# Zero rows of a cache gradient in four unequal transfers, and gradient rows fetched back one by one

## The chip, the cores and the metric

The kernel runs on one core of a Trainium2 chip. The metric is the device time of one execution in microseconds, as the median of several runs. One execution is also recorded by the hardware profiler; its times are counted from the start of the profile's span.

## What is computed

The reference runs a small decode step for one token (a row `x` of 1024 values) through two rounds of two layers, and returns the output and its gradients by all inputs but one bias:

```
x = x + A(layernorm(x));  x = x + B(layernorm(x));  x = x + A(layernorm(x));  x = x + B(layernorm(x))

A: q = x @ wq                          # wq 1024 x 4096, 32 heads of 128
   k, v = the last 4096 of 32768 rows of k_cache, v_cache   # 4 heads, each for 8 query heads
   o = softmax(q k^T / sqrt(128)) v;  return o @ wo         # wo 4096 x 1024
B: h = x @ w1 + b1;  return (h * tanh(softplus(h))) @ w2    # w1 1024 x 3584, w2 3584 x 1024
```

All of it is bfloat16. The returned gradients of `k_cache` and `v_cache` (`out_2`, `out_3`) have the full shape, 4 heads x 32768 rows x 128. Only the last 4096 rows of a head can differ from zero; the 28,672 rows before them (7.3 MB for each head, 58.7 MB in all) are zeros that the kernel has to write. The gradients of the four weight matrices (`out_4` to `out_6`, `out_8`) are outer products of two pairs of rows each.

## The kernel before

The weights come in through a ring of eight SBUF slots of 1 MB (`Ring`), filled by transfers on SyncE's queue (SP) in an order that is written down ahead; a slot is filled again when its user has released it (L71). The forward pass of both rounds comes first, then the backward pass from the last layer to the first. Each weight is read by TensorE, partly after turning 128x128 blocks on TensorE (L489) and copying them back with VectorE and ScalarE. The last pass of the backward chain is `attn_bwd(0, ...)`, which goes through `wo` and then through `wq` (hooks `do1`, `dp1`, `dq1`, `dn1` are called within it). Behind it the outer products are made: `work` takes units of the queues in `todo`, each unit a matmul of two rows by two rows into PSUM (L1078, and L1129 for the caches), an evacuation to SBUF, and `store` sends the piece to HBM on SP's queue (L1050, L1055).

**The zeros.** `zt` is an SBUF tile of 128 partitions x 4096 values (8 KB per partition) that is set to zero at 110 us. The list `zjobs` cuts the zero rows of each head into seven pieces of 1 MB, in which each of the 128 partitions writes one run of 8 KB. The first piece is written half by SP earlier on, and its other half is put at the end of the list. `zeros(n, after)` takes the next `n` pieces and issues one transfer for each on GpSimd's queue (POOL, L265), behind a one-value copy (L260) that waits for `after`. The calls are spread over the kernel by hand: 56 pieces in all, 55 whole ones and the half one. The last calls are `zeros(2, ...)` in `dn1` at t = 3 and `zeros(4)` behind `attn_bwd(0, ...)`, which issues three whole pieces and the half one.

**The gradient rows.** The outer products want rows, while the backward pass holds columns. `put_by` turns the columns of OC, NA, NB and AC (both rounds, "l" = 0 and 1, beside each other) and stores them in small HBM tensors `dr_OC`, `dr_NA`, `dr_NB`, `dr_AC`. `take_back(name, base, off, step)` in `do1` at c = 1 fetches them into `ROWS` (a part of the tile W1): row l to partition base + l, as n runs of 256 bytes, with n = 32 for OC, 8 for NA and NB, 28 for AC. With `step=2`, the default, one transfer brings both rows; AC uses `step=1`, one transfer for each row. All five are issued on POOL's queue (L836). The rows that are made later (`rowize`, `rowize_f`) go by the same queue (L1041), 8 runs or 7 runs to a transfer. `twins` then copies pairs of rows to other partitions on SP's queue (L1070).

Of the kernel before, what the change touches and what calls it, by code (L numbers as in the profile page):

```python
# [15 lines left out]
P = 128  # L16
HQ = 32
DH = 128
# [3 lines left out]
G = 4  # L22
W = 4096
TD = D // P
TF = F // P
# [68 lines left out]
def kernel(  # L94
# [22 lines left out]
    nc = tc.nc  # L117
# [3 lines left out]
    ZR = Sk - W  # L121
# [9 lines left out]
    def sb(shape, dtype, name):  # L131
        return keep.tile(shape, dtype, name=name)
# [24 lines left out]
    ZC = 4096  # L157
    zt = sb([P, ZC], BF16, "zt")
# [36 lines left out]
    for hi in range(4):  # L195
        r = slice(32 * hi, 32 * hi + 32)
# [10 lines left out]
    AC = sb([P, TF, 2], BF16, "AC")  # L207
# [38 lines left out]
    zjobs = []  # L246
    for out_t in (out_2, out_3):
        for g in range(G):
            dst = out_t[0, g, 0:ZR, :].rearrange("(p r) d -> p (r d)", p=P).rearrange("p (r c) -> p r c", c=ZC)
            for k in range(dst.shape[1]):  # L250
                zjobs.append(dst[:, k, :])
    zjobs.reverse()

    pz = sb([1, 16], FP32, "pz")
# [2 lines left out]
    def zeros(n, after=None):  # L257

        if after is not None and zjobs:
            nc.gpsimd.tensor_copy(pz[0:1, pz_n[0] % 16:pz_n[0] % 16 + 1], after[0:1, 0:1])  # L260
            pz_n[0] += 1
        for _ in range(n):
            if zjobs:
                dst = zjobs.pop()
                nc.gpsimd.dma_start(dst, zt[:, 0:dst.shape[1]])  # L265


    KEEP_Q = (5, 6, 7)
# [96 lines left out]
    def to_eight(bank, buf):  # L365

        nc.vector.transpose(buf[:, 0:256], bank[:, 0:256])
        return buf[:, 0:256].rearrange("p (g m) -> p g m", m=32)[:, :, 0]
# [434 lines left out]
    def last_da(k):  # L803

        for c in (5, 6):
            if k == 0:
                da_dots(c)
            else:
                ring.release(("2", 0, c))
        if k:  # L810
            nc.gpsimd.memset(zt[:], 0.0)
            zeros(1)

    def wo_hook1(c):
        if c == 0:
            zeros(7, OC[:, 0, 1:2])
        if c:
            conv(1)
# [10 lines left out]
        DR[name] = dram.tile([2 * n, P], BF16, name=f"dr_{name}")  # L829
        nc.sync.dma_start(DR[name][:], r)  # L830

    def take_back(name, base, off, step=2):
        r = DR[name][:].rearrange("(n l) p -> l n p", l=2)
        to = ROWS[base:base + 2, off:off + r.shape[1] * P].rearrange("l (n p) -> l n p", p=P)
        for l in range(0, 2, step):
            nc.gpsimd.dma_start(to[l:l + step], r[l:l + step])  # L836

    x3, st3, sA1 = attn_fwd(1, x2, st2, False, wo_hook1, last_da)
    put_by("OC", OC, HQ)
    put_by("NA", NA, TD)  # L840
    zeros(8, x3)
    sB1 = mlp_fwd(1, x3, st3, lambda: conv(1, "A"))
    put_by("NB", NB, TD)
# [26 lines left out]
    def rowize_f():  # L870

        b = big().bitcast(BF16)
        for l in range(2):
            for k in range(4):
                nc.tensor.transpose(b[0:7, (4 * l + k) * P:(4 * l + k + 1) * P],
                                    DHC[:, :, l].rearrange("p (c k) -> p k c", k=4)[:, k], ident_bf[:])
        nc.scalar.copy(rf.rearrange("c (l p k) -> c l p k", l=2, k=4), b[0:7].rearrange("c (l k p) -> c l p k", l=2, k=4))
        for l in range(2):
            rows_out.append((ROWS[64 + l:65 + l, NOFF:NOFF + F].rearrange("o (c j) -> o c j", j=512),
                             rf[:, 512 * l:512 * l + 512]))  # L880
# [133 lines left out]
    ROWS = W1S[:, 0:5120]  # L1014
    NOFF = 1024
# [11 lines left out]
    def rowize(cols, n, base, off):  # L1027

        b = big().bitcast(BF16)
        nc.tensor.transpose(b[0:2 * n, 0:P], cols[:].rearrange("p n l -> p (n l)"), ident_bf[:])  # L1030
        k = rt_n[0]
        rt_n[0] += 1
        nc.scalar.copy(rt[0:2 * n, k, :], b[0:2 * n, 0:P])
        for l in range(2):
            rows_out.append((ROWS[base + l:base + l + 1, off:off + n * P].rearrange("o (t p) -> o t p", p=P),
                             rt[l:2 * n:2, k, :]))

    def rows_go(queue):

        while rows_out:  # L1040
            queue.dma_start(*rows_out.pop(0))  # L1041
# [144 lines left out]

    def do1(c):
        if c == 1:
            take_back("AC", 96, NOFF, 1)
            take_back("OC", 32, NOFF)  # L1190
            take_back("NB", 64, 0)
            take_back("NA", 0, 0)
        if c == 4:
            y = to_eight(YR, RT.rearrange("p a t s -> p (a t s)")[:, 0:512].bitcast(FP32))
            nc.vector.tensor_tensor(out=x4[:], in0=y, in1=x3[:], op=ALU.add)
        if c == 5:
            rowize(GA, TD, 32, 0)
            rowize(GB, TD, 96, 0)
            rows_go(nc.gpsimd)
            zeros(2)  # L1200
        if c == 6:
            rowize_f()
            rows_go(nc.gpsimd)
# [13 lines left out]
    def dn1(t):  # L1217
# [6 lines left out]
        if t == 5:  # L1224
            todo[0].append(units_cols(0, 8, out_4))

    g0_rest = attn_bwd(0, sA0, g1, ("o", 3), ("q", 3), (), dict(do=do1, dp=dp1, dq=dq1, dn=dn1))
    zeros(4)
    stage_free.extendleft(ring_t[:, i, :] for i in range(8))
    stage_free.extendleft(lent)  # L1230

# [50 lines left out]
```

## Time and profile before

| What | Value |
|---|---|
| median of 3 runs | 450.72 us (450.44 to 450.92) |
| the profiled execution | 450.31 us |
| its span | 448.5 us |
| granted TensorE clock, mean | 0.668 |
| DMA traffic in the span | 181.40 MB, mean 404 GB/s |
| busy: PE, DVE, ACT, POOL | 70%, 58%, 47%, 10% |
| the 55 whole zero pieces | 1024 KB each, 20.7 us from issue to landing (median) |

The page of the profile gives busy time by engine, the span in 40 slices of 11.2 us, the DMA queues, and the costliest groups of instructions. q1 is the queue of SP, q0 that of POOL, q10 that of ACT. "DMA" is the mean busy share of the 16 DMA engines of the core. A transfer is cut into packets (8 KB or less here), dealt out over the DMA engines, and each engine ends its part with a 4-byte packet that counts up the transfer's semaphore. A line number such as L265 is a line of the kernel as printed above.

### The profile page before, as it was taken

The numbers are of one execution on the slowest core, as the hardware profiler recorded it, in microseconds if no ns is written. First come the engines' busy times: TensorE is split into PE (matmuls) and PEld (weight loads), VectorE is DVE, ScalarE is ACT, GpSimd is POOL, SyncE is SP. The second block draws the span as 40 slices with busy tenths as digits, with TensorE's granted clock in tenths as the row PEclk, the third lists the DMA queues.
The fourth block names the chain that finished last, engine by engine and source line by source line (L and its number), as shares of the span: only waits on it lengthen the run. The fifth ranks groups of instructions, "written<-read, shape, count | busy, mean of one in ns | idle before, by whom it ended". The sixth has DMA issues, their size and how long they took to land.

```text
span 448.5 us, 12849 instructions
## 1 busy us (share of the span) xinstructions
PE 314.8 (70%) x5681; PEld 243.3 (54%) x5681; DVE 262.2 (58%) x516; ACT 209.4 (47%) x238; POOL 44.5 (10%) x94
## 2 busy tenths in 40 slices
PE   3835542565698797987987666798877888899600
PEld 3735532445685696986986545798862222234300
DVE  4504746368551664864477447654478998998600
ACT  2501101011058576861474341561348999999700
POOL 1000000001232212102101003023220000000000
PEclk9955555556559799986799657957685555555555
DMA  8999999999999999999999999999999899999994
GB/s 336 422 420 420 419 419 418 418 355 425 400 422 421 422 422 416 397 422 422 424 422 422 427 423 419 405 410 388 405 397 412 347 411 416 416 420 411 409 406 192
DMA packets 30057, 181.40 MB, mean 404 GB/s; under 512 B 3954, under 2 KB 5162, under 8 KB 12082
## 3 DMA queue, kind: packets, MB, share of 16 engines
q1 hardware_dynamic: 21478, 122.30, 66.6%
q0 software_dynamic: 8432, 58.26, 31.5%
q8 instruction: 44, 0.72, 0.6%
q14 instruction: 11, 0.09, 0.0%
q10 hardware_dynamic: 92, 0.02, 0.0%
HBM read 81.84 MB, written 98.62 MB: 402 GB/s over the span
## 4 chain that ended last, share of the span: by engine, by line
DMA 40%; PE 31%; DVE 13%; ACT 5%; issue 4%; SPq 0%; ACTq 0%; DVEq 0%
DMA ring<-in_B_w_dram 13%; PE BIG L489 10%; DMA W<-in_A_wo_dram 9%; DMA ring<-in_A_wq_dram 7%; DMA ring<-in_A_wo_dram 5%; DMA W<-in_B_w_dram 4%; PE TP L508 4%; PE wide L1129 4%; ACT ring L316 3%; PE wide L1078 3%; DVE ring L313 3%; DMA W<-in_A_k_cache_dram 2%; DVE W L313 2%; PE BIG L667 2%; PE MV L956 2%
## 5 line engine op out<-in xcount | busy, mean ns | idle before, releaser
L316 ACT COPY ring<-BIG 128x1024 bf16<-128x1024 bf16 x52 | 51.4, 1014 | 50.0 <-PE BIG L489 30.2
L1078 PE MATMUL wide<-W 2*128 2x512 bf16 x240 | 53.1, 597 | 9.7 <-ACT ring L316 2.4
L489 PE MATMUL BIG<-ident_bf,ring 128*128 128x128 bf16 x672 | 54.5, 234 | 2.0 <-issue 1.2
L489 PEld LDWEIGHTS <-ring 128*128 128x128 bf16 x768 | 51.6, 107 | 3.4 <-issue 2.7
L466 DVE CUSTOM_DVE_ANT_0 junk<-ring,SC 128x1024 bf16<-128x1024 bf16 x32 | 38.9, 1215 | 11.0 <-DMA ring<-in_B_w_dram 10.6
L1078 PEld LDWEIGHTS <-W 2*128 2x128 bf16 x240 | 12.8, 102 | 46.3 <-issue 45.4
L508 PEld LDWEIGHTS <-ring 128*128 128x128 bf16 x864 | 29.9, 98 | 11.7 <-issue 6.3
L316 ACT CAST ring<-wide 128x1024 bf16<-128x1024 f32 (+1 forms) x37 | 34.5, 1015 | 1.1 <-PE wide L1078 1.1
L265 POOL DMA_DIRECT2D out_dram<-zt x56 | 29.9, 538 | 48.8 <-DMA out_dram<-zt 47.9
L313 DVE CAST ring<-wide 128x1024 bf16<-128x1024 f32 (+1 forms) x27 | 31.3, 1198 | 2.8 <-PE wide L1078 2.7
L316 ACT COPY KT<-BIG 128x1024 bf16<-128x1024 bf16 x22 | 21.6, 1007 | 21.8 <-PE BIG L667 19.9
L313 DVE COPY ring<-BIG 128x1024 bf16<-128x1024 bf16 x32 | 21.8, 689 | 15.1 <-PE BIG L489 12.5
L466 DVE CUSTOM_DVE_ANT_0 junk<-ring,DSX 128x1024 bf16<-128x1024 bf16 x24 | 29.4, 1224 | 0.8
L489 PE MATMUL BIG<-ident_bf,W 128*128 128x128 bf16 x280 | 26.9, 255 | 3.1 <-DMA W<-in_A_wo_dram 2.7
L316 ACT COPY W<-BIG 128x1024 bf16<-128x1024 bf16 x20 | 20.1, 1014 | 11.8 <-PE BIG L489 11.6
L551 PE MATMUL MV<-NA,ring 128*128 128x1 bf16 x512 | 15.3, 165 | 13.4 <-DMA ring<-in_A_wq_dram 12.1
L489 PEld LDWEIGHTS <-W 128*128 128x128 bf16 x288 | 21.6, 123 | 3.5 <-DMA W<-in_A_wo_dram 2.9
L551 PEld LDWEIGHTS <-ring 128*128 128x128 bf16 x512 | 14.7, 104 | 14.2 <-DMA ring<-in_A_wq_dram 12.8
L1129 PE MATMUL wide<-W 32*128 32x256 bf16 x128 | 19.7, 403 | 1.5 <-DVE KT L313 0.9
L316 ACT CAST KT<-wide 128x1024 bf16<-128x1024 f32 x19 | 19.1, 1030 | 1.6 <-PE wide L1129 1.1
L316 ACT CAST W<-wide 128x1024 bf16<-128x1024 f32 x16 | 16.0, 1024 | 6.6 <-PE wide L1078 6.2
L354 PE MATMUL YR<-ring,AC 128*32 128x256 bf16 x208 | 10.9, 367 | 11.1 <-DMA ring<-in_B_w_dram 8.7
(279 smaller groups left out, 524.5 us busy)
## 6 DMA issues: line engine op xcount, KB each, us to landing
out_dram<-zt POOLq DMA_DIRECT2D x55, 1024.0 KB, 20.7
ring<-in_A_wq_dram SPq DMA_DIRECT2D x24, 1024.0 KB, 12.8
ring<-in_A_wo_dram SPq DMA_DIRECT2D x14, 1024.0 KB, 19.0
ring<-in_B_w_dram SPq DMA_DIRECT2D x13, 1024.0 KB, 18.9
W<-in_A_wo_dram SPq DMA_DIRECT2D x10, 1024.0 KB, 19.9
out_dram<-ring SPq DMA_DIRECT2D x15, 512.0 KB, 11.1
W<-in_B_w_dram SPq DMA_DIRECT2D x8, 896.0 KB, 18.4
out_dram<-ring SPq DMA_DIRECT2D x5, 1024.0 KB, 12.3
```

Source lines behind the costliest of these rows:

```text
L265: nc.gpsimd.dma_start(dst, zt[:, 0:dst.shape[1]])
L313: nc.vector.tensor_copy(dst, src)
L316: nc.scalar.copy(dst, src)
L354: nc.tensor.matmul(bank[32 * j:32 * j + 32, 0:n].rearrange("p (g a) -> p g a", a=m.shape[-1]), lhsT=vec.to_broadcast([P, 32]), rhs=m, star ...
L466: nc.vector.tensor_tensor_reduce(out=out, in0=a, in1=vec, scale=1.0, scalar=acc if i else 0.0, op0=ALU.mult, op1=ALU.add, accum_out=acc)
L489: nc.tensor.transpose(b[:, i * P:(i + 1) * P], block(w, i) if block else w[:, i * P:(i + 1) * P], ident_bf[:])
L508: nc.tensor.matmul(out, lhsT=w[:, i * P:(i + 1) * P], rhs=rhs_of(i), start=fresh[0], stop=last and i == n - 1, skip_group_check=True)
L551: nc.tensor.matmul(q_ps[:, h:h + 1], lhsT=ch[:, h * P:(h + 1) * P], rhs=NA[:, t, l:l + 1], start=(k == 0 and h == 0), stop=(k == TD - 1), ...
L667: nc.tensor.transpose(b[:, i * P:(i + 1) * P], T[:, g, 8 * b8 + i, :], ident_bf[:])
L956: nc.tensor.matmul(dq_ps[:, g_ * 8:g_ * 8 + 8], lhsT=KT[:, g_, t, :], rhs=DSX[:, c:c + 8], start=(g_ == 0 and t == 0), stop=(t == TS - 1), ...
L1078: nc.tensor.matmul(b[:, 512 * i:512 * i + 512], lhsT=R[at:at + 2, lo:lo + P], rhs=R[at:at + 2, ro + 512 * i:ro + 512 * i + 512], start=Tru ...
L1129: nc.tensor.matmul(b[:, k * 256:(k + 1) * 256], lhsT=RT[32 * g:32 * g + 32, a, tp, :], rhs=YS[32 * g:32 * g + 32, :], start=True, stop=Tru ...
```

## The change

For the last of the eight heads (`out_3`, g = 3) the zero rows are cut differently: 896 units of 32 rows (8 KB each). The first 512 units (4 MB) are set aside as `zless`; the other 384 make three ordinary pieces of 1 MB. So `zjobs` is four pieces shorter, and the call `zeros(4)` at the end becomes `zeros_less()`, which writes the 512 units with four transfers: from 4 partitions (0, 4, 8, 12) 33 units each, from partition 16 17 units, from 3 partitions (20, 24, 28) 33 each, and from 8 partitions (64, 68, ... 92) 33 each. Each partition of the tile of zeros is read again and again for its units. The half piece, last in the list, is now issued by the call in `dn1`.

`take_back` issues one transfer for each row; AC's row of 28 runs is fetched in two, of 24 and of 4 runs. That makes ten transfers in place of five, and the parameter `step` goes.

```diff
     for out_t in (out_2, out_3):
         for g in range(G):
-            dst = out_t[0, g, 0:ZR, :].rearrange("(p r) d -> p (r d)", p=P).rearrange("p (r c) -> p r c", c=ZC)
-            for k in range(dst.shape[1]):
-                zjobs.append(dst[:, k, :])
+            rest = out_t[0, g, 0:ZR, :]
+            if (out_t, g) != (out_3, G - 1):
+                dst = rest.rearrange("(p r) d -> p (r d)", p=P).rearrange("p (r c) -> p r c", c=ZC)
+            else:
+                units = rest.rearrange("(u r) d -> u (r d)", r=ZC // DH)
+                zless, dst = units[0:4 * P], units[4 * P:].rearrange("(r p) c -> p r c", p=P)
+            zjobs += [dst[:, k, :] for k in range(dst.shape[1])]
...
+    def zeros_less():
+
+        at = 0
+        for k, p, n in ((4, 0, 33), (1, 16, 17), (3, 20, 33), (8, 64, 33)):
+            nc.gpsimd.dma_start(zless[at:at + k * n].rearrange("(k n) c -> k n c", k=k),
+                                zt[p:p + 4 * k:4, None, :].to_broadcast([k, n, ZC]))
+            at += k * n
...
-    def take_back(name, base, off, step=2):
+    def take_back(name, base, off):
+
         r = DR[name][:].rearrange("(n l) p -> l n p", l=2)
-        to = ROWS[base:base + 2, off:off + r.shape[1] * P].rearrange("l (n p) -> l n p", p=P)
-        for l in range(0, 2, step):
-            nc.gpsimd.dma_start(to[l:l + step], r[l:l + step])
+        n = r.shape[1]
+        for l in range(2):
+            to = ROWS[base + l:base + l + 1, off:off + n * P].rearrange("o (n p) -> o n p", p=P)
+            for a, b in ((0, 24), (24, n)) if n == TF else ((0, n),):
+                nc.gpsimd.dma_start(to[:, a:b], r[l:l + 1, a:b])
...
-            take_back("AC", 96, NOFF, 1)
+            take_back("AC", 96, NOFF)
...
-    zeros(4)
+    zeros_less()
```

## The prediction

> **What bounds the kernel now.** I read the page first: the row of the 16 DMA engines, the queues, the byte count.
>
> ```profile
> span 448.5 us, 12849 instructions
> ...
> DMA  8999999999999999999999999999999899999994
> ...
> DMA packets 30057, 181.40 MB, mean 404 GB/s; under 512 B 3954, under 2 KB 5162, under 8 KB 12082
> ...
> q1 hardware_dynamic: 21478, 122.30, 66.6%
> q0 software_dynamic: 8432, 58.26, 31.5%
> ```
>
> The DMA engines are full in 38 of 40 slices, and thin out only in the last. The kernel is bound by 181.4 MB of traffic, of which POOL's zeros (q0) are 58 MB. The change moves the same bytes, so it can win only where engines stand idle: at the end. The table by stage, cut fine there (columns: stretch, its length, busy time of PE, weight load, DVE, ACT and POOL, clock, share of the 16 DMA engines, GB/s), shows it:
>
> ```profile
> 440.00:442.00 2.00, 0.00 (x0) 0.00 (x0) 0.00 (x0) 0.00 (x0) 0.00 (x0) 0.50 1.03 410
> 442.00:442.50 0.50, 0.00 (x0) 0.00 (x0) 0.00 (x0) 0.00 (x0) 0.00 (x0) 0.50 0.52 205
> 442.50:443.00 0.50, 0.00 (x0) 0.00 (x0) 0.00 (x0) 0.00 (x0) 0.00 (x0) 0.50 0.14 57
> 443.00:443.50 0.50, 0.00 (x0) 0.00 (x0) 0.00 (x0) 0.00 (x0) 0.00 (x0) 0.50 0.06 25
> 443.50:444.00 0.50, 0.00 (x0) 0.00 (x0) 0.00 (x0) 0.00 (x0) 0.00 (x0) 0.50 0.06 25
> 444.00:445.00 1.00, 0.00 (x0) 0.00 (x0) 0.00 (x0) 0.00 (x0) 0.00 (x0) 0.50 0.07 29
> 445.00:446.00 1.00, 0.00 (x0) 0.00 (x0) 0.00 (x0) 0.00 (x0) 0.00 (x0) 0.50 0.06 25
> 446.00:447.00 1.00, 0.00 (x0) 0.00 (x0) 0.00 (x0) 0.00 (x0) 0.00 (x0) 0.50 0.07 29
> ```
>
> No engine computes. Up to 442 all 16 DMA engines move 410 GB/s, 25.6 each; from 443 to 447 the rate is 25 to 29 GB/s, a share of 0.06: **one DMA engine works alone** for 4 us, the other 15 are done.
>
> The trace also keeps every DMA packet with start, duration, size and queue, but without its engine. The last ones give the exact end: 4096-byte packets of 159 ns, starting 155 ns apart (a packet starts 3 to 4 ns before the one ahead of it ends), the last ending at 447.16. Eleven engines end between 442.15 and 442.35, the next to last at 443.07. From the last packet to the span's end (448.54) are 1.38 us, and from the span to the execution's time (450.31) 1.77.
>
> **Which engine it is.** By that 3 to 4 ns rule packets can be chained, each 16th of a transfer in its order. From 200 to 281 us the chains are unbroken: in one, an 8192-byte packet takes 323.3 ns in the mean and 69 take over 330; in the other 15 the mean is 309.0 to 315.4, with at most 2 over 330. So one engine is slow, and it drags its zeros behind it: of POOL's last old transfer, 15 sixteenths are through at 347 and eight packets run alone from 352.5 to 354.7.
>
> The same chains show how POOL's transfers are dealt out. Transfers with one outer dimension always go to the same engines: the two 28-row fetches of AC to the same 14, two rows each, the four 8-row moves of GA and GB at 301 us to the same eight. Transfers with two outer rows (OC, NB, NA) take two engines each, and each the next two: six different ones, all among those eight. The slow engine has one of NA's two shares: the fifth or sixth in turn.
>
> **The change, part by part.**
>
> *Unequal shares.* Behind the last pass of wq, before: four transfers, 3.5 MB; after: 512 units of 8 KB in groups of 4, 1, 3 and 8 partitions, 33 units each, but 17 for the lone one. One more half-size job falls to the call ahead, so the two calls move 5.5 MB together as before. Even dealing of 512 units is 32 per engine. A unit took 309 ns and starts 305 to 306 after the one ahead. If each partition is one engine in turn from the first, the fifth has 15 units less: 15 x 0.306 = 4.59 us; the rest one more, 0.31. The slow engine then ends at 447.16 - 4.59 = 442.57, and late next is the engine of 443.07, at 443.07 + 0.31 = 443.38. The end moves by 447.16 - 443.38 = 3.78 us. Nothing is won earlier: the DMA share is 1.01 to 1.03 in all stages from 360 on.
>
> *Issues.* Four for four; one took 0.53 to 0.69 us on POOL, in the view of tile zt. They have 17 to 264 units, not 128; by count that is 0.1 to 1.4 us each. POOL has no work behind them, and at 331.6 its queue still holds transfers that land up to 355.5. I take 0; up to 2 us late costs nothing while that backlog lasts.
>
> *One partition read 33 times.* No row shows it. Below, 0: a packet read one partition before, too. Above, the slow engine's 323 instead of 309 ns: 33 x 14 = 0.46 us. I take 0, which is nearest: same packet size and direction.
>
> *Row fetches.* Five issues become ten. POOL's timeline (start, length, what, idle before it and its releaser):
>
> ```profile
> 276.92 1.04 POOL L836 DMA_DIRECT2D W<-dr_AC  x2 [5.29 <-DMA ring<-in_A_wo_dram]
> 278.00 0.70 POOL L836 DMA_DIRECT2D W<-dr_OC  x1
> 278.69 0.60 POOL L836 DMA_DIRECT2D W<-dr_NB  x1
> 279.28 0.56 POOL L836 DMA_DIRECT2D W<-dr_NA  x1
> 298.22 2.06 POOL L1041 DMA_DIRECT2D W<-W  x4 [18.38 <-ACT W L1033]
> ```
>
> Five more at 0.52 to 0.70 us are 3 us, into 18.38 us of idle. POOL has eight completion semaphores in turn, so the ninth fetch waits for the first to land (14.8 us after its issue, 291.7), the tenth likewise: POOL is free near 293. Behind it wait L1041's moves, which wait for ACT until 298.22, and SP's copies (L1070), first at 305.23. On the slow engine a data packet and its semaphore alternate with q1's 8 KB packets, 0.65 us per fetch; ten end near 297.5. Cost 0; without the cover each us behind 298.22 would delay the twins and the first stores.
>
> What the fetches do is to leave the turn alone: no transfer with two rows is left. If the turn starts each execution where it started here, the shares begin at the first engine.
>
> **Sum.** 450.31 - 3.78 = 446.53 against the profiled execution. That one lies 0.41 under the median (450.72), so I predict 446.9.
>
> **The rivals.**
>
> *A. The short share is the slow engine's*: 446.9; with the costs above up to 447.6, down to 446.3 if the spread among the others closes too. For it: the lag (447.16 - 442.3 = 4.9 us) is 16 units of 0.306, what the lone share lacks; the pair of NA. Against: fifth or sixth is open, and so is how 17 rows of one partition are dealt. 0.50.
>
> *B. The 17 units are dealt like the 28 rows of AC*, two each over nine engines from the first; then 4, 3 and 8 engines follow in turn, and the sixteenth has none. The slow engine has 35 units in place of 32: 3 x 0.306 = 0.92 us later, 451.6. It decides as soon as one outer row of 17 is treated as the AC fetches were, and they show just that. This is the rival on the other side. 0.25 with kindred ones (17 units beside 33 on one engine: 442.3 + 18 x 0.306 = 447.8, 0.65 later, 451.4).
>
> *C. The short share falls on another engine*: the sixth was the slow one, or the turn stands elsewhere (before moves it by six engines per execution; if that outlives an execution, the starting point is any). The slow engine has 33: 0.31 later, 451.0, no change. 0.20.
>
> *D. A cost I take as 0 appears*, the fetches above all: 451.5 and more, 0.05.
>
> Two rules of the Trainium skill, page "DMA: Bandwidth & Descriptors", bear on this. Its section "Why a DMA increments its semaphore by 16 and not by 1" says a transfer uses the largest k up to 16 that divides its slowest dimension, on k consecutive engines from a round-robin cursor, but that some POOL copies deal ⌈partitions/16⌉ to each. By the first, 17 rows sit on one engine (case A); by the second the sum is B's. The trace disagrees with the first for AC: 14 engines, the cursor not moved. The section "Latency and other measured facts" says engines 7 and 15 are usually the slow ones; by that the fifth share would miss, as in C. The trace has one slow engine only, in NA's pair, which contradicts it if the turn starts at the first engine.
>
> **How the numbers follow.** A is likeliest: 446.9, its own range 446.3 to 447.6. Half of the rest is on the other side, so the range goes over B: 446.3 to 451.7. Within 0.2% (0.9 us, what a measurement can tell apart) of 450.72 lies C and a small part of B; slower are most of B and D. Faster 0.50, same 0.22, slower 0.28.
>
> **What would show it.** A: the lone stretch at 25 GB/s behind 442 gone or under 1 us, the DMA share near 1 up to some 443, span 444.8. B or C: the stretch as long or longer; in B one engine's share runs out some 9 us before the others, so the rate falls by a sixteenth near 433. Ten fetches between 277 and 293 and L1041 still at 298 confirm the cover; if L1041 waits for a landing, D. The prediction is wrong in its base if the slow engine is no property of the chip but changes from run to run.

## The result, and the profile after

| | before | after |
|---|---|---|
| median | 450.82 us (450.44 to 451.04, 4 runs) | 454.44 us (454.11 to 454.82, 4 runs) |
| the profiled execution | 450.31 us | 454.82 us |
| its span | 448.5 us | 453.0 us |
| last packet ends at | 447.16 us | 451.69 us |

The changed kernel is slower: ratio 1.0082, 95% interval 1.0064 to 1.0099. That is 7.5 us above the predicted 446.9 and 2.7 above the top of its range, 451.7. The lines of the page of after that answer to those shown of before:

```profile
span 453.0 us, 12855 instructions
...
DMA  8999999999999999999999999999999799999993
GB/s 337 420 421 418 419 422 417 418 357 424 404 421 419 417 417 413 392 421 425 422 422 423 422 421 386 414 416 421 416 384 369 277 407 416 417 418 412 408 408 156
DMA packets 31305, 181.40 MB, mean 400 GB/s; under 512 B 5182, under 2 KB 6418, under 8 KB 13330
...
q1 hardware_dynamic: 21478, 122.30, 66.1%
q0 software_dynamic: 9680, 58.27, 31.5%
```

The bytes are the same, and the packets of SP's queue (q1) too. POOL's queue has 1248 packets more, nearly all of them small: the whole kernel has 1228 more under 512 bytes. Slice 32 (351 to 362 us) falls to 277 GB/s. The table by stage of after (columns as in the prediction) goes through that stretch and the end:

```profile
340.00:345.00 5.00, 2.91 (x18) 0.98 (x18) 2.94 (x8) 3.31 (x6) 0.00 (x0) 0.50 1.01 380
345.00:350.00 5.00, 4.33 (x19) 0.99 (x17) 4.82 (x5) 5.00 (x7) 0.00 (x0) 0.50 1.01 359
350.00:355.00 5.00, 3.90 (x22) 1.05 (x20) 5.00 (x5) 4.79 (x7) 0.00 (x0) 0.50 0.93 346
355.00:358.00 3.00, 2.69 (x13) 0.65 (x10) 2.67 (x4) 3.00 (x4) 0.00 (x0) 0.50 0.79 303
358.00:362.00 4.00, 3.78 (x25) 1.40 (x23) 3.15 (x4) 3.72 (x6) 0.00 (x0) 0.50 0.56 213
362.00:367.00 5.00, 4.14 (x21) 0.93 (x18) 5.00 (x5) 5.00 (x6) 0.00 (x0) 0.50 0.96 379
...
444.00:446.00 2.00, 0.00 (x0) 0.00 (x0) 0.00 (x0) 0.00 (x0) 0.00 (x0) 0.50 0.76 305
446.00:448.00 2.00, 0.00 (x0) 0.00 (x0) 0.00 (x0) 0.00 (x0) 0.00 (x0) 0.50 0.14 57
448.00:450.00 2.00, 0.00 (x0) 0.00 (x0) 0.00 (x0) 0.00 (x0) 0.00 (x0) 0.50 0.09 37
450.00:453.00 3.00, 0.00 (x0) 0.00 (x0) 0.00 (x0) 0.00 (x0) 0.00 (x0) 0.50 0.03 14
```

The same view of before, for the first stretch:

```profile
340.00:345.00 5.00, 3.82 (x21) 1.26 (x18) 3.70 (x8) 3.62 (x7) 0.00 (x0) 0.50 1.01 410
345.00:350.00 5.00, 3.82 (x20) 0.92 (x16) 4.55 (x4) 5.00 (x6) 0.00 (x0) 0.50 1.03 408
350.00:355.00 5.00, 4.08 (x21) 1.01 (x19) 4.83 (x6) 4.79 (x7) 0.00 (x0) 0.50 0.92 362
355.00:358.00 3.00, 2.62 (x14) 0.68 (x14) 2.67 (x3) 3.00 (x4) 0.00 (x0) 0.50 0.64 258
358.00:362.00 4.00, 3.69 (x23) 1.42 (x21) 3.37 (x4) 3.85 (x5) 0.00 (x0) 0.50 1.02 402
```

Two things are to be seen. From 340 to 350 the DMA share is 1.01 in after and 1.01 to 1.03 in before, but the rate is 380 and 359 GB/s in place of 410 and 408: the engines are as busy and move less. And the dip to 258 GB/s that before has at 355 to 358, where the slow engine's last zeros land (355.5), comes later and lasts longer in after. By the rows shown, after moves 7.19 MB from 340 to 362 and before 8.28: 1.1 MB less, which is 2.7 us at 408 GB/s. At the end the lone stretch is still there: fourteen of the 16 engines are done by 446.4, one by 448.9, and the last packet ends at 451.69. In before fifteen are done by 443.1 and the last packet ends at 447.16. So most of the 4.5 us is not a longer lone stretch: fourteen of the others end some 3 us later too.

The trace tells where the 512 units went. POOL's four transfers were issued at 326.5, 327.2, 328.7 and 331.5. Each of the 16 engines counts up a transfer's semaphore when it is through with its part; sorted by time:

| transfer | engines done by 336 us | the others |
|---|---|---|
| 4 partitions x 33 units | 11 | 341.7, 343.6, 344.4, 344.6, 347.1 |
| 1 x 17 | 11 | 342.5, 345.0, 346.7, 346.9, 348.3 |
| 3 x 33 | 9 | six from 349.6 to 353.3, one at 361.6 |
| 8 x 33 | 1 | fourteen from 346.5 to 359.8, one at 366.8 |

In before each transfer has 15 engines together and one 5 to 8 us behind. Here that late engine is the one of 361.6 and 366.8: it carries 33 units of the group of three, and it is not among the four engines of the first transfer. One engine is through with all four transfers by 333.9: it got nothing, just as the sixteenth in rival B. The count of small packets fits it (below, first experiment).

POOL's timeline of after, for the fetches:

```profile
279.44 2.04 POOL L852 DMA_DIRECT2D W<-dr_AC  x4 [5.08 <-DMA ring<-in_A_wo_dram]
281.47 1.04 POOL L852 DMA_DIRECT2D W<-dr_OC  x2
284.86 0.52 POOL L852 DMA_DIRECT2D W<-dr_NB  x1 [2.35 <-issue]
289.83 0.50 POOL L852 DMA_DIRECT2D W<-dr_NB  x1 [4.45 <-DMA out_dram<-zt]
290.52 1.15 POOL L852 DMA_DIRECT2D W<-dr_NA  x2 [0.19 <-issue]
297.06 1.97 POOL L1057 DMA_DIRECT2D W<-W  x4 [5.39 <-DVE W L326]
```

Ten issues, the last done at 291.7 us. The one longer wait within them is for an older zero piece (289.83), not for the first fetch. L1057 (L1041 of before) waits for VectorE until 297.06, not for a landing: the cover held.

### The profile page after: what moved, and what is told of

Its sections match the earlier page's. It is cut to its first block, busy times and chain, and to the rows that moved or that the text cites. A ratio compares the mean times of both kernels' runs of the same rounds, so it can differ in the third digit from the quotient of the medians.

```text
span 453.0 us, 12855 instructions
## 1 busy us (share of the span) xinstructions
PE 310.0 (68%) x5681; PEld 238.5 (53%) x5681; DVE 261.3 (58%) x516; ACT 209.1 (46%) x238; POOL 47.3 (10%) x99
## 3 DMA queue, kind: packets, MB, share of 16 engines
q0 software_dynamic: 9680, 58.27, 31.5%
## 5 line engine op out<-in xcount | busy, mean ns | idle before, releaser
L502 PEld LDWEIGHTS <-ring 128*128 128x128 bf16 x768 | 50.9, 106 | 3.4 <-issue 2.7
L521 PEld LDWEIGHTS <-ring 128*128 128x128 bf16 x864 | 29.6, 97 | 12.8 <-issue 6.7
L269 POOL DMA_DIRECT2D out_dram<-zt x52 | 27.8, 538 | 40.4 <-DMA out_dram<-zt 39.6
L502 PE MATMUL BIG<-ident_bf,W 128*128 128x128 bf16 x280 | 23.9, 233 | 0.9 <-issue 0.5
L564 PEld LDWEIGHTS <-ring 128*128 128x128 bf16 x512 | 14.7, 104 | 13.9 <-DMA ring<-in_A_wq_dram 12.5
L502 PEld LDWEIGHTS <-W 128*128 128x128 bf16 x288 | 19.1, 113 | 1.9 <-DMA W<-in_A_wo_dram 0.9
```

Of the source, the lines that this page charges most:

```text
L502: nc.tensor.transpose(b[:, i * P:(i + 1) * P], block(w, i) if block else w[:, i * P:(i + 1) * P], ident_bf[:])
L521: nc.tensor.matmul(out, lhsT=w[:, i * P:(i + 1) * P], rhs=rhs_of(i), start=fresh[0], stop=last and i == n - 1, skip_group_check=True)
L564: nc.tensor.matmul(q_ps[:, h:h + 1], lhsT=ch[:, h * P:(h + 1) * P], rhs=NA[:, t, l:l + 1], start=(k == 0 and h == 0), stop=(k == TD - 1), ...
```

## Experiments

**Theory P.** The 17 units were dealt as in rival B. That transfer did not move the turn (the engine with which the next transfer of several rows begins), so the groups of three and eight began one engine early. Each engine of these two groups then read its units out of a partition that is not in its own share of SBUF, and that is what makes them slow. "Own" means the partitions that an engine gets in an ordinary piece of 1 MB. The Trainium skill, page "DMA: Bandwidth & Descriptors", section "The descriptor swizzle", gives the map for a 1 MiB transfer to 128 partitions, in which every engine has eight fixed ones: the engine is the cluster of four that the partition lies in, 0 to 7 for partitions 0 to 31 and again for 32 to 63, and 8 to 15 for 64 to 95 and again for 96 to 127. So the change's partitions 0, 4, 8, 12, then 16, then 20, 24, 28, then 64 to 92 name each engine's own partition once, if each transfer takes the next engines in turn. The experiments equal_own and equal_swapped below agree with this map.

**Rivals:** the fetches cost the time (the prediction's D); reading one partition over and over costs it, whichever engine does it (R); and, for single runs, those that their expectations name.

Every edit below is to after, unless it says otherwise. All ratios are to before, which ran beside each on the same chip. fetch_only, zeros_only, equal_own and equal_swapped ran on one chip (before 450.64, 19 runs); three_from_16, short_pair, short_pair_25 and old_fetch_pair on another (450.98, 7 runs); own_17_124, own_17_16 and after_17_124 on a third (450.66, 13 runs); short_pair_11 on a fourth (450.59, 7 runs).

**The fetches alone (fetch_only).** The kernel before with the new take_back; the zeros as in before.

> The row-by-row fetches alone, with the zeros as before. Theory P (the time is lost in the zeros: the slow engine gets 33 + 2 of the 512 units, and reads them from a partition of another engine's share of SBUF, 450 to 470 ns a unit where 309 is usual): the fetches cost nothing, 450.8 within 0.5. Rival F (the ten fetches hold up POOL or the slow engine): 452 or more, part or all of the 3.6 us.

Measured: 450.25 us (449.63 to 452.57), ratio 0.9998 [0.9985, 1.0011]. The fetches cost nothing; D falls. Its page gives the packets of POOL's queue without the unequal zeros:

```profile
q0 software_dynamic: 8576, 58.26, 31.5%
```

After has 9680, so the four transfers bring 1104 small packets that the four ordinary ones had not. They have 4 bytes: in each transfer an engine without a share gets as many of them as another engine has units. Group of 4: 12 engines x 33 = 396. Group of three: 13 x 33 = 429. Group of eight: 8 x 33 = 264. These make 1089, and 15 are left for the 17 units. On one engine the 17 would have left 15 x 17 = 255; dealt out two at a time over nine engines, 16 x 2 - 17 = 15. That fits rival B's dealing to the packet. The count alone would also fit one unit on each of 16 engines and a second on one of them; against that speaks AC in before, whose 2 x 28 runs of 256 bytes stand in the trace as 28 packets of 512, two runs to an engine. The 15 speak against the rule of the largest divisor, by which 17 sit on one engine, and for the exception to it; both are rules of the Trainium skill that the prediction weighed (page "DMA: Bandwidth & Descriptors", section "Why a DMA increments its semaphore by 16 and not by 1").

**The zeros alone (zeros_only).** After with the old take_back.

> The four unequal transfers alone, with the fetches as before, which leave the turn six engines on. Theory P: the shares of 33 fall to engines 7 to 10, then 11 to 13, then 14 to 16 and 1 to 5 in turn, the sixth has none. If the slow engine is the fifth, it has 35 units from a partition of another share of SBUF: 452 to 455. If it is the sixth, it has 2 units at most, ends some 9 us earlier, and the engine next to last sets the end: 447 to 448. Rival R (reading one partition over and over is slow on any engine): 454 either way.

Measured: 457.90 us (456.74 to 459.37), ratio 1.0175 [1.0155, 1.0196]: the loss is in the zeros, and it is larger than expected. The old fetches with two rows leave the turn six engines on, so that still more groups read foreign partitions; 46 zero packets between 350 and 362 us took 468 ns in the mean, and nine between 330 and 339 us took 1.1 to 2.6 us each. The size of this loss I had not right.

The run also bears on which engine is the slow one. By its dealing the sixth engine alone has no share of 33. One engine's count of all four transfers is complete at 338.6 us, before the slow engine is through with the older pieces (340.8). That one is the sixth, so the slow engine is not the sixth here. short_pair below, on another chip, has it in the pair of the fifth and sixth; if it is the same engine on both chips, it is the fifth.

**Equal shares from own partitions (equal_own), and from swapped ones (equal_swapped).** Each engine gets 32 units; in the second kernel only the order of the two groups differs, so the first eight engines read the partitions of the last eight.

```diff
-        for k, p, n in ((4, 0, 33), (1, 16, 17), (3, 20, 33), (8, 64, 33)):
+        for k, p, n in ((8, 0, 32), (8, 64, 32)):      # equal_own
+        for k, p, n in ((8, 64, 32), (8, 0, 32)):      # equal_swapped
```

> Two transfers of 8 partitions with 32 units each (partitions 0, 4, ... 28, then 64, 68, ... 92), fetches row by row: each engine has 32 units, as in the kernel before, read again and again from one partition, that of its own share of SBUF. Theory P: 450.8 within 0.6, units of the slow engine near 309 to 330 ns. Rival R (one partition read over and over is the price): 453.5 to 455.

> The same two transfers in the other order: partitions 64, 68, ... 92 first, then 0, 4, ... 28. Equal shares again, but each engine now reads the partition of the engine eight places on. Theory P: slower than the run with own partitions by 2 to 4 us, 453 to 455, with units of 420 ns and more on the slow engine once the other stores are under way. Rival R: the same time as with own partitions.

Measured: equal_own 450.70 us (449.81 to 451.33), ratio 1.0003 [0.9993, 1.0012]; equal_swapped 455.82 us (454.15 to 458.27), ratio 1.0123 [1.0087, 1.0159]. The table by stage of equal_own:

```profile
345.00:350.00 5.00, 4.48 (x19) 1.12 (x19) 4.82 (x6) 5.00 (x7) 0.00 (x0) 0.50 1.03 405
350.00:355.00 5.00, 3.92 (x22) 1.06 (x20) 4.67 (x6) 4.79 (x7) 0.00 (x0) 0.50 0.71 281
355.00:358.00 3.00, 2.69 (x13) 0.64 (x11) 3.00 (x3) 3.00 (x5) 0.00 (x0) 0.50 0.94 374
358.00:362.00 4.00, 3.78 (x22) 1.38 (x22) 3.16 (x4) 3.72 (x5) 0.00 (x0) 0.50 1.02 401
```

And of equal_swapped:

```profile
345.00:350.00 5.00, 4.34 (x20) 1.07 (x19) 4.82 (x5) 5.00 (x7) 0.00 (x0) 0.50 1.02 381
350.00:355.00 5.00, 3.92 (x23) 1.10 (x22) 4.76 (x5) 4.79 (x6) 0.00 (x0) 0.50 0.77 281
355.00:358.00 3.00, 2.69 (x11) 0.53 (x8) 2.91 (x3) 3.00 (x5) 0.00 (x0) 0.50 0.28 96
358.00:362.00 4.00, 3.78 (x24) 1.49 (x23) 3.16 (x4) 3.72 (x5) 0.00 (x0) 0.50 0.45 171
```

Both read one partition 32 times per engine. With own partitions the time is that of before; with foreign ones the signs of after come back enlarged: full share at a lower rate up to 350, then a long stretch at a share of 0.28 to 0.45. R falls, P stands: 5.1 us hang on which partition an engine reads. The trace's zero packets of 8 KB say it by themselves (mean of those that start from 350 to 362 us, when by the counts above most should be the slow engine's; longest of those from 342 to 350):

| kernel | mean, 350 to 362 | longest, 342 to 350 | last packet |
|---|---|---|---|
| before | 315 ns (5 packets) | 348 ns | 447.16 |
| equal_own | 321 (10) | 334 | 446.67 |
| equal_swapped | 480 (23) | 845 | 452.75 |
| after | 490 (17) | 968 | 451.69 |
| three_from_16 | 316 (21) | 2384 | 450.45 |
| own_17_124 | 319 (14) | 3115 | 448.20 |
| own_17_16 | 316 (14) | 2496 | 449.83 |
| after_17_124 | 406 (25) | 2502 | 449.72 |
| short_pair | 319 (9) | 340 | 443.00 |

**The group of three put right (three_from_16).** With partitions 16, 20 and 24 the fifth to seventh engines read their own.

```diff
-((4, 0, 33), (1, 16, 17), (3, 20, 33), (8, 64, 33))
+((4, 0, 33), (1, 16, 17), (3, 16, 33), (8, 64, 33))
```

> The changed kernel with one number changed: the group of three reads partitions 16, 20, 24 in place of 20, 24, 28, so that engines 5 to 7 read from their own shares of SBUF (the group of eight still reads one place off on engines 8 to 15). The slow engine keeps its 33 + 2 units. Theory P (the slow engine's foreign partition was 3.2 us of the loss, its 3 units too many 0.9): 451.7, between 451.2 and 452.3, its units at 309 to 335 ns. Rival Q (the foreign partition costs through the other engines too, so the group of eight keeps the loss): 453.5 or more.

Measured: 453.69 us (453.53 to 454.29), ratio 1.0065 [1.005, 1.008]. The slow engine's packets are back at 316 ns, as P says, but only 0.9 us of after's 3.6 us are regained (by the ratios, 0.0017 x 450.8 = 0.8, and their intervals overlap). The expected 451.7 was wrong and rival Q's 453.5 right. The table shows where the loss may lie now: packets of up to 2.4 us between 342 and 350. Partition 16 is now read by one engine 33 times and by nine engines for the 17 units.

**What the 17 units cost (own_17_124, own_17_16, after_17_124).** The first two put every group of 33 on own partitions, so that only the 17 units are read by other engines, from partition 124 (in the share of the engine that has no work) or from partition 16 (in the share of the fifth). The third changes nothing in after but this partition.

```diff
-((4, 0, 33), (1, 16, 17), (3, 20, 33), (8, 64, 33))
+((8, 0, 33), (1, 124, 17), (4, 64, 33), (3, 80, 33))      # own_17_124
+((8, 0, 33), (1, 16, 17), (4, 64, 33), (3, 80, 33))       # own_17_16
+((4, 0, 33), (1, 124, 17), (3, 20, 33), (8, 64, 33))      # after_17_124
```

> The same numbers of units per transfer as the change, in an order that lets every engine read its own partition: 8 from partition 0, then 4 from 64, then 3 from 80, 33 units each; the 17 units come from partition 124, of the one engine that has no other share. The slow engine has 33 + 2 units as in the changed kernel. Theory P (count costs 3 x 0.306 us, the rest of the loss is foreign partitions): 451.7, between 451.2 and 452.2. Rival V (the dealing as such costs more, one engine without a share, or the empty packets): 453 to 454.5.

> The same, but the 17 units come from partition 16 as in the change: nine engines read two units each from the slow engine's share of SBUF. Theory W (this is what was left of the loss when the group of three read its own partitions): 453 to 454, that is 1.3 to 2.3 us over the run with partition 124; the 15 units that the others take there are 4.6 us of that engine's time at most. Rival: 451.7, no difference, and the rest lies with the group of eight.

> The changed kernel with only the 17 units moved to partition 124. Theory W: 452 to 453. Rival (the groups of three and eight carry the loss): 454.4 within 0.5.

Measured: 451.32 us, ratio 1.0015 [1.0005, 1.0024]; 453.42 us, 1.0067 [1.0052, 1.0082]; 452.80 us, 1.0053 [1.0036, 1.0069]. One line of the table by stage of own_17_124 and one of own_17_16:

```profile
345.00:350.00 5.00, 4.34 (x21) 1.03 (x19) 4.83 (x5) 5.00 (x7) 0.00 (x0) 0.50 0.92 324
```

```profile
345.00:350.00 5.00, 2.75 (x14) 0.67 (x14) 3.58 (x4) 4.27 (x5) 0.00 (x0) 0.50 0.84 246
```

Where equal_own has 405 GB/s, own_17_124 has 324 and own_17_16 has 246: the same 17 units of 8 KB, 139 KB in all, cost 2.1 us more from the one partition than from the other. own_17_124, with its groups of 33 on own partitions, is 0.66 us over before. That is near the 0.92 that the prediction gave for the slow engine's three more units; the run does not separate them from what the 17 units cost from partition 124.

The runs split after's loss of 3.6 us in steps: 0.7 for the unequal shares with every group of 33 on own partitions (own_17_124); 1.5 more when the groups of three and eight read one place off (after_17_124, 452.80 - 451.32); 1.5 more when the 17 units come from partition 16 (after, 3.6 us over before, against after_17_124's 2.1). This last step is not clear of the noise: by the ratios it is 1.3, and their intervals overlap. In the other layout the same partition costs 2.1 (own_17_16 against own_17_124), and there the intervals are apart. The steps do not simply add: putting the group of three alone right brought 0.8 and moved reads onto the crowded partition. What the group of eight costs by itself was not tried.

**The intended gain (short_pair, short_pair_25).** A group of two rows is dealt to the next two engines, as OC, NB and NA showed. So a pair takes the fifth and sixth engine, one of which is the slow one, and every group stays on its own partitions.

```diff
-((4, 0, 33), (1, 16, 17), (3, 20, 33), (8, 64, 33))
+((4, 0, 34), (2, 16, 18), (2, 24, 34), (8, 64, 34))      # short_pair
+((4, 0, 33), (2, 16, 25), (2, 24, 33), (8, 64, 33))      # short_pair_25
```

> Groups of 4, 2, 2 and 8 partitions with 34, 18, 34 and 34 units, each engine reading its own partition, fetches row by row: no group of one, so all shares move the turn; engines 5 and 6 have 18 units, the others 34. Theory P: the slow engine is one of the two and ends 14 x 0.306 = 4.3 us earlier, the others 2 x 0.306 = 0.6 later; the end is that of the next to last, 443.07 + 0.6, so 450.7 - 3.5 = 447.2, between 446.7 and 448. Rival S (the slow engine is not in the pair): 451.3, slower by 0.6. Rival T (the end is not set by that engine's zeros): 450.7.

> The same with 33, 25, 33 and 33 units. Theory P: the slow engine ends 7 x 0.306 = 2.1 us earlier and still sets the end, at 445.0: 448.6, between 448.1 and 449.2. Rival S: 451.0. Rival T: 450.7.

Measured: short_pair 446.22 us (446.19 to 446.32), ratio 0.9898 [0.9883, 0.9912]; short_pair_25 448.49 us (448.04 to 448.55), ratio 0.9945 [0.9931, 0.996]. The end of short_pair, by stage:

```profile
438.00:440.00 2.00, 0.00 (x0) 0.00 (x0) 0.00 (x0) 0.00 (x0) 0.00 (x0) 0.50 0.86 348
440.00:442.00 2.00, 0.00 (x0) 0.00 (x0) 0.00 (x0) 0.00 (x0) 0.00 (x0) 0.50 0.34 139
442.00:444.00 2.00, 0.00 (x0) 0.00 (x0) 0.00 (x0) 0.00 (x0) 0.00 (x0) 0.50 0.03 12
```

With 14 units less than the even 32 on the slow engine the last packet ends 4.2 us earlier (14 x 0.306 = 4.3), with 7 less 1.8 us (2.1). The gain that case A counted on is real; it needs the right dealing, with every group on its own partitions. The other 15 engines end between 437.9 and 441.8 here, the slow one at 443.0.

**Two shares of 11 (short_pair_11).** The same, levelled further: `((4, 0, 35), (2, 16, 11), (2, 24, 35), (8, 64, 35))`.

> As the version with the two short shares of 18 units, but the two short shares have 11 units and the other 14 have 35; all read partitions of the engine's own. In that version the slow engine ended at 443.0 and the other 15 between 440.2 and 441.8. Theory P (the slow engine's number of units sets the end until another engine is later): the slow engine has 7 units less, 7 x 0.306 = 2.1 us, and ends at 440.9; the others one more, 0.3, so the latest of them ends at 442.1 and sets the end. Last packet 442.1, time 0.9 us below that version: 445.3, ratio to before 0.988. Rival X (what is left of the lone stretch does not come from the number of units but from the last transfers themselves, so fewer units gain nothing more): last packet 442.8 to 443.3, time 446.0 to 446.6.

Measured: 444.94 us (444.44 to 446.22), ratio 0.9884 [0.9861, 0.9907], the fastest of all. Its end by stage:

```profile
438.00:440.00 2.00, 0.00 (x0) 0.00 (x0) 0.00 (x0) 0.00 (x0) 0.00 (x0) 0.50 0.88 360
440.00:441.00 1.00, 0.00 (x0) 0.00 (x0) 0.00 (x0) 0.00 (x0) 0.00 (x0) 0.50 0.33 135
441.00:442.00 1.00, 0.00 (x0) 0.00 (x0) 0.00 (x0) 0.00 (x0) 0.00 (x0) 0.50 0.02 8
```

All 16 engines end between 437.9 and 441.3, and no long stretch at 25 GB/s is left. That it is faster than short_pair the trace suggests, by 1.7 us at the last packet; the two ratios' intervals overlap, and the two ran on different chips.

**The pair with the old fetches (old_fetch_pair).** The old take_back leaves the turn six engines on; the groups are put in the order that this asks for.

```diff
-((4, 0, 33), (1, 16, 17), (3, 20, 33), (8, 64, 33))
+((2, 24, 34), (8, 64, 34), (4, 0, 34), (2, 16, 18))      # and take_back as before
```

> The fetches as in the kernel before (the turn stands at engine 7 behind them), and the groups in the order that fits that: 2 partitions from 24 with 34 units, 8 from 64 with 34, 4 from 0 with 34, 2 from 16 with 18. Each engine again reads its own partition and engines 5 and 6 have 18 units. Theory P with the turn starting at the first engine in each execution: 447.2 as the run with row-by-row fetches, so that these were not needed. Rival U (the turn is kept over executions, and moves by 6 + 16 in each): times that scatter between 447 and 458 from run to run.

Measured: 447.75 us (446.81 to 447.89), ratio 0.9924 [0.9906, 0.9943]. No zero packet behind 338 us is over 345 ns, so every group met its own engines; and the four executions lie within 1.1 us of each other, where rival U had them scatter from 447 to 458. So the turn starts at the first engine in each execution, and the rows need not be fetched one by one at all. Why it is 1.5 us slower than short_pair is open; the short pair comes last in POOL's queue there.

## Why the prediction was wrong

- **What bounds the kernel: right.** DMA, and at the end one slow engine alone (37 slices of the page stand at 9, not the 38 that the prediction counts as full). Taking units from that engine moved the end by what they weigh. The base held too: with even shares one engine lags in every execution profiled.
- **Row fetches, cost 0: right**: fetch_only 0.9998. POOL was free at 291.7 us, worked out at near 293; what it waited for on the way was an older zero piece and not the first fetch.
- **The start of the turn, first engine in each execution: right** (equal_own against equal_swapped; old_fetch_pair). The slow engine is in the pair that the fifth and sixth share form, and by zeros_only it is likely the fifth, as A had it. So A failed by the dealing of the 17 units, and not by the place of the slow engine.
- **Which case: wrong.** The step that failed is "If each partition is one engine in turn from the first, the fifth has 15 units less". A transfer with one outer row is not dealt that way. The runs showed two units to an engine over nine engines, the turn not moved: the slow engine had 33 + 2 units, and the groups behind began one engine early. The trace of before had shown as much with AC: 28 rows, 14 engines, two each, the turn not moved. I had that in hand as rival B, with its dealing right to the unit, and gave case A 0.50 and B 0.25 only because 16 missing units would have matched the lag so well. That a number fits what a change would need is no sign of how the hardware deals. One reading was wrong on the way: AC's 14 engines do not speak against the largest divisor, as the prediction says, for 14 is the largest divisor of 28 up to 16, and the eight engines of the 8-row moves fit it too. Only the turn that AC left where it was spoke against it. No row of before told the two rules apart by the number of engines; the 17 units of after do.
- **B's size: wrong**, and this is the mis-sized term: "One partition read 33 times ... I take 0", bounded above by 0.46 us. For an engine's own partition 0 is right (equal_own 1.0003). But the bound took for granted that any partition is as near as any other. In B's own dealing the turn is not moved, so the groups behind read one place off, and nine engines read one partition; I did not carry the dealing through to what each engine reads. So B's +0.9 us became +3.6, of which own_17_124 puts 0.7 to the unequal shares themselves. In before no engine reads zeros from another's share, so there was no row for this, and 14 ns a packet was no upper end.
- **Four for four issues: right** in the work on POOL. The 1104 empty packets were not foreseen. The prediction's sign of B, the rate falling by a sixteenth near 433 us, did not come: the table by stage has 407 GB/s at 430 to 434 us in after, 406 in before.

What stays open: how the reads of one partition by nine engines reach the slow engine (the trace names no engine for a packet, and the longest packets, 3.1 us in own_17_124, are not in the kernel that loses most); why after, with the same 17 units from partition 16, has no packet over 968 ns; whether the slow engine is the fifth on every chip; the group of eight's own part; why zeros_only loses as much as it does.

## What to carry to other kernels

Where transfers end on one lagging DMA engine, giving it fewer units pays by what they weigh: here 1.0 to 1.2% for 14 to 21 units of 8 KB. But before relying on a share, count: the semaphore's 16 increments and the 4-byte packets tell how many engines a transfer went to and when each was done, and a transfer with a single outer row was dealt otherwise here than one with two or more. And let each engine read a re-read tile from its own partitions; check the packet durations of the first run, where 309 and 470 ns are easily told apart.

## What the runs showed of the hardware

- Where engines read 8 KB packets from partitions of another engine's share, these took 468 to 490 ns in the mean (zeros_only, equal_swapped, after; 406 in after_17_124) in place of 315 to 321 (before, equal_own), from 350 to 362 us. While many did so the DMA share stayed at 1.0 and the rate fell (equal_swapped 381 GB/s, equal_own 405, from 345 to 350 us).
- In kernels where nine engines read the same partition for the 17 units, single 8 KB packets took over 1 us: 9 of them in own_17_124, 15 in own_17_16, up to 3.1 us. It is not so in each: after has none over 968 ns. equal_own has none over 334 ns from 338 us on.
- An engine without a share in a POOL transfer still gets 4-byte packets, as many as the largest share has units (1104 in after by this count, and as many on record).
- A transfer from POOL with one outer row of n runs was dealt out with ⌈n/16⌉ runs to an engine, always from the same engine on, and left the turn where it was: 28 runs on 14 engines and 8 on eight in before, 17 on nine in after. One with 2, 3, 4 or 8 outer rows took as many engines from the turn and moved it on (before, after, equal_own, short_pair). The turn starts anew in each execution (old_fetch_pair).
- One of the 16 DMA engines, of the fifth and sixth from the start of the turn, was slower than the others in before: 323 ns for an 8 KB packet where the others took 309 to 315 from 200 to 281 us.
